# A Fourier-mixing and squared-ReLU feed-forward kernel: from radix 2 to radix 4, with two engines' work moved

## The chip, the cores and the metric

One core of one Trainium2 chip. The metric is the device time of one execution in microseconds (us). Executions of one kernel agree within about 0.3%. A ratio is the mean time of one kernel's fast runs over that of the other's fast runs of the same rounds, so it isn't quite the ratio of the medians that stand beside it; a 95% interval follows it in brackets. Differences to the kernel before are taken within the same rounds.

## The reference

```python
x: (8, 3008, 256) fp32
X = np.fft.fft(np.fft.fft(x, axis=1), axis=2).real    # over the sequence, then over the width
t = X.reshape(24064, 256)
h = np.maximum(t @ w_in, 0.0)                          # w_in  (256, 2048)
out = h * h @ w_out                                    # w_out (2048, 256)
```

## The kernel before

A batch goes through four steps. **Stage 1** multiplies the sequence by cosine and sine tables on the Tensor engine (PE), after the sequence has been split by radix 2 into even and odd rows: two halves of 1504 rows, 12 blocks of 128 each. As 753 output columns are needed and a tile has 384, there are two column tiles, so 16 passes over the 8 batches. **Combine** puts the two halves together with twiddle factors (10 element-wise operations a half on the Vector engine, DVE). **dmix** does the transform over the width on PE. Then come the **feed-forward chains**, 64 in all, of 384 tokens each:

```python
ps_pq   = tile_pool(bufs=4, PSUM)    # stage 1
ps_misc = tile_pool(bufs=2, PSUM)    # dmix, pso
ps_h    = tile_pool(bufs=2, PSUM)    # psh          -> all 8 banks are used
...
for (xt, rev, ...) in chains:                             # 64 times
    h2 = h2p.tile([P, NFC, KT], F16)
    for fc in range(NFC):                                 # 16 "hidden blocks" of 128 hidden units
        psh = ps_h.tile([P, KT], F32)
        for dpc in range(NDC):                            # 2 matmuls, 384 columns
            matmul(psh, win16[...], rhs, ...)
        h1 = h1p.tile([P, KT], F16)                       # 4 buffers
        nc.scalar.activation(h1, psh, AF.Relu)            # ACT, out of PSUM
        nc.vector.tensor_tensor(h2[:, fc, :], h1, h1, op=ALU.mult)      # DVE, square
    for tck in range(ntc):                                # 3 groups of 128 tokens
        pso = ps_misc.tile([P, D], F32)
        for fc in range(NFC):                             # 16 matmuls, 256 columns
            matmul(pso, h2[:, fc, c0 : c0 + P], wout16[:, fc, :], ...)
        nc.scalar.activation(osb, pso, AF.Copy, scale=HS * HS)
        dma(out[...], osb[...])
```

The dmix and feed-forward part of a pass is written after stage 1 of the next one. The order in which PE meets its matmuls isn't the order of this text: it is set when the kernel is built, and it is fixed from then on.

## Time and profile before

| | before |
|---|---|
| time, median | 1118.51 us (13 runs; the four that the prediction had: 1117.62) |
| span, granted PE clock | 1117.4 us, 0.998 |
| PE matmuls: stage 1, dmix, psh, pso | 1536, 256, 2048, 3072 |
| at 0.163 us (384 columns) and 0.115 us (256 columns) | 979 us of pure PE work |
| span less that work | 138 us "lost" |

One view more is needed: the output matmuls (pso) that PE runs in one piece at the end of each feed-forward chain, from the timeline of PE (start in us, duration, group, count).

```profile
566.88 4.26 PE L157 MATMUL pso<-wout,h 128*128 128x256 f16 x35
579.18 4.26 PE L157 MATMUL pso<-wout,h 128*128 128x256 f16 x35
591.49 4.26 PE L157 MATMUL pso<-wout,h 128*128 128x256 f16 x35
```

A chain has 48 pso. In the built order 35 of them stand at the end, so only 13 are left to fill the time in which PE waits for a PSUM buffer of the hidden product. The chains follow each other every 12.30 us, and their own work is 32 x 0.163 + 48 x 0.115 = 10.74 us.

### The profile page before, as it was taken

The numbers are of one execution on the slowest core, as the hardware profiler recorded it, in microseconds if no ns is written. First come the engines' busy times: TensorE is split into PE (matmuls) and PEld (weight loads), VectorE is DVE, ScalarE is ACT, GpSimd is POOL, SyncE is SP. The second block draws the span as 40 slices with busy tenths as digits, with TensorE's granted clock in tenths as the row PEclk, the third lists the DMA queues.
The fourth block names the chain that finished last, engine by engine and source line by source line (L and its number), as shares of the span: only waits on it lengthen the run. The fifth ranks groups of instructions, "written<-read, shape, count | busy, mean of one in ns | idle before, by whom it ended". The sixth has DMA issues, their size and how long they took to land.

```text
span 1117.4 us, 18635 instructions
## 1 busy us (share of the span) xinstructions
PE 1056.5 (95%) x6912; PEld 656.4 (59%) x6912; DVE 633.5 (57%) x1601; ACT 586.2 (52%) x1303; POOL 83.8 (8%) x130
## 2 busy tenths in 40 slices
PE   1699999999999999999999999999999999999998
PEld 0256656666666666656666665656566666665655
DVE  2586564746547474574747456474654747456454
ACT  5537446263653727476262645626365472635666
POOL 5340010100001010020101001010000100000000
PEclk9999999999999999999999999999999999999999
DMA  9062040412304040141403204041221400000101
GB/s 217 6 89 52 30 70 29 71 34 49 55 32 72 28 71 29 35 65 39 69 31 54 47 30 70 28 70 36 47 52 32 67 30 15 28 28 15 37 29 32
DMA packets 78235, 53.63 MB, mean 48 GB/s; under 512 B 3648, under 2 KB 77888, under 8 KB 77888
## 3 DMA queue, kind: packets, MB, share of 16 engines
q0 software_dynamic: 51216, 25.69, 18.0%
q1 hardware_dynamic: 26928, 26.75, 7.2%
q8 instruction: 54, 0.88, 0.3%
q14 instruction: 37, 0.30, 0.1%
HBM read 53.48 MB, written 24.64 MB: 70 GB/s over the span
## 4 chain that ended last, share of the span: by engine, by line
PE 86%; ACT 5%; DVE 4%; issue 2%; POOL 1%; DMA 1%; POOLq 0%; DVEq 0%; ACTq 0%
PE psh L144 33%; PE pso L157 28%; PE ps L211 21%; ACT h L147 3%; DVE h L148 2%; PE psY L128 2%; PE psY L124 2%; DVE m L98 1%; ACT u L92 1%; DMA win<-in_moe_w_in_dram 1%; POOL t L96 1%; ACT eco L102 1%; ACT win L67 0%; DVE xtF L132 0%; POOL t L94 0%
## 5 line engine op out<-in xcount | busy, mean ns | idle before, releaser
L147 ACT ACTIVATE h<-psh 128x384 f16<-128x384 f32 x1024 | 468.3, 490 | 302.9 <-PE psh L144 227.3
L148 DVE TENSOR_TENSOR h<-h 128x384 f16<-128x384 f16 x1024 | 359.4, 358 | 342.7 <-ACT h L147 316.5
L157 PE MATMUL pso<-wout,h 128*128 128x256 f16 x3072 | 478.5, 273 | 8.3 <-DVE h L148 2.2
L157 PEld LDWEIGHTS <-h 128*128 128x128 f16 x3072 | 285.0, 97 | 128.3 <-DVE h L148 34.8
L144 PEld LDWEIGHTS <-win 128*128 128x128 f16 x2048 | 197.7, 97 | 168.8 <-issue 79.7
L144 PE MATMUL psh<-xtF,win 128*128 128x384 f16 x1024 | 231.9, 325 | 8.8 <-ACT h L147 4.3
L144 PE MATMUL psh<-xtR,win 128*128 128x384 f16 x1024 | 231.9, 323 | 5.9 <-ACT h L147 1.0
L160 ACT ACTIVATE osb<-pso 128x256 f32<-128x256 f32 x192 | 73.2, 383 | 176.6 <-PE pso L157 176.5
L211 PEld LDWEIGHTS <-xe 128*128 128x128 f16 (+1 forms) x768 | 76.9, 100 | 74.4 <-DMA xe<-in_x_dram 17.4
L211 PEld LDWEIGHTS <-xo 128*128 128x128 f16 (+1 forms) x768 | 75.5, 98 | 67.2 <-issue 16.4
L211 PE MATMUL ps<-eco,xe 128*128 128x384 f16 (+1 forms) x384 | 76.1, 337 | 30.7 <-ACT eco L102 28.1
L211 PE MATMUL ps<-eco,xo 128*128 128x384 f16 (+1 forms) x384 | 79.5, 332 | 2.9 <-DMA xo<-in_x_dram 2.9
L211 PE MATMUL ps<-esi,xe 128*128 128x384 f16 (+1 forms) x384 | 79.0, 335 | 0.0
L211 PE MATMUL ps<-esi,xo 128*128 128x384 f16 (+1 forms) x384 | 74.6, 332 | 0.0
L189 POOL DMA_DIRECT2D xe<-in_x_dram x16 | 17.4, 1089 | 685.1 <-PE ps L211 566.7
L216 DVE TENSOR_TENSOR t1c<-ps,cbc 128x384 f32<-128x384 f32 x32 | 17.7, 552 | 78.2 <-PE ps L211 77.5
L132 DVE TENSOR_TENSOR xtF<-y1sb,psY 128x384 f16<-128x384 f32 x64 | 35.2, 550 | 6.1 <-PE psY L128 2.6
L131 DVE COPY y1sb<-psY 128x384 f32<-128x384 f32 x64 | 35.1, 549 | 3.5 <-PE psY L124 3.5
L133 DVE TENSOR_TENSOR xtR<-y1sb,psY 128x384 f16<-128x384 f32 x64 | 35.0, 546 | 0.0
L98 DVE SCALAR_TENSOR_TENSOR m<-t,u 128x384 f32<-128x384 f32 (+1 forms) x28 | 15.7, 564 | 29.9 <-POOL t L96 29.9
L92 ACT ACTIVATE u<-krow,mvec 128x384 f32<-128x384 f32 x24 | 14.8, 616 | 27.9 <-DVE m L98 27.9
L218 DVE TENSOR_TENSOR t2c<-ps,sbc 128x384 f32<-128x384 f32 x32 | 17.7, 552 | 13.1 <-PE ps L211 13.1
(47 smaller groups left out, 352.5 us busy)
## 6 DMA issues: line engine op xcount, KB each, us to landing
out_dram<-osb SPq DMA_DIRECT2D x144, 128.0 KB
xe<-in_x_dram POOLq DMA_DIRECT2D x16, 704.0 KB, 7.3
xo<-in_x_dram POOLq DMA_DIRECT2D x16, 704.0 KB, 7.2
win<-in_moe_w_in_dram SPq DMA_DIRECT2D x1, 2048.0 KB
out_dram<-osb SPq DMA_DIRECT2D x16, 127.0 KB
out_dram<-osb SPq DMA_DIRECT2D x16, 113.0 KB
out_dram<-osb SPq DMA_DIRECT2D x16, 112.0 KB
wout<-in_moe_w_out_dram POOLq DMA_DIRECT2D x1, 1024.0 KB, 12.5
```

The costliest lines, as they stand in the source:

```text
L92: nc.scalar.activation(u, src_row, AF.Copy, bias=0.0, scale=scal_ap)
L98: nc.vector.scalar_tensor_tensor(out=m, in0=t2, scalar=-float(nmod), in1=u, op0=ALU.mult, op1=ALU.add)
L124: nc.tensor.matmul(psY1, ccos[:, dc, dpc * P : (dpc + 1) * P], cp[:, dc, :], start=(dc == 0), stop=(dc == NDC - 1))
L131: nc.vector.tensor_copy(y1sb, psY1)
L132: nc.vector.tensor_tensor(xtF[:, dpc, :], y1sb, psY2, op=ALU.subtract)
L133: nc.vector.tensor_tensor(xtR[:, dpc, :], y1sb, psY2, op=ALU.add)
L144: nc.tensor.matmul(psh, win16[:, dpc, fc * P : (fc + 1) * P], rhs, start=(dpc == 0), stop=(dpc == NDC - 1))
L147: nc.scalar.activation(h1, psh, AF.Relu)
L148: nc.vector.tensor_tensor(h2[:, fc, :], h1, h1, op=ALU.mult)
L157: nc.tensor.matmul(pso, h2[:, fc, c0 : c0 + P], wout16[:, fc, :], start=(fc == 0), stop=(fc == NFC - 1))
L160: nc.scalar.activation(osb, pso, AF.Copy, bias=0.0, scale=HS * HS)
L211: nc.tensor.matmul(psu, xs, tabs[mc][0:np_, :], start=(mc == 0), stop=(mc == NMC - 1))
```

## The change

The intent: halve the work of stage 1 by radix 4 (four parts of 752 rows, 6 blocks each, one column tile, 8 passes), and pay for it with a larger combine (8 evictions on ACT and 34 element-wise operations a half), which goes to the idle GpSimd engine (POOL) from the third batch on. Relu and square change engines: relu, out of PSUM, goes to DVE and the square, out of SBUF, to ACT. Room is made with fewer buffers and by giving the fp32 input weights the place of h2.

```diff
-    M = S // 2
+    M = S // R                       # R = 4
...
-    xtp = ...(name="xtp", bufs=5)
+    fsb = ...(name="fsb", bufs=2)
+    gtp = ...(name="gtp", bufs=1)
+    xtp = ...(name="xtp", bufs=9)
...
-    win32 = const.tile([P, NDC, F], F32, name="win32")
+    win32 = h2p.tile([P, NDC, F], F32, name="win32", tag="big")
...
-                nc.scalar.activation(h1, psh, AF.Relu)
-                nc.vector.tensor_tensor(h2[:, fc, :], h1, h1, op=ALU.mult)
+                nc.vector.tensor_scalar(out=h1, in0=psh, scalar1=0.0, scalar2=None, op0=ALU.max)
+                nc.scalar.activation(h2[:, fc, :], h1, AF.Square)
...
-    for kt in range(NKT):            # 2 column tiles
-        for b in range(B):
+    for b in range(B):
...
-                # combine: 10 operations, DVE, out of PSUM
+                for (r, trig), psu in ps4.items():
+                    t_ = fsb.tile([P, KT], F32, ...)
+                    nc.scalar.copy(t_, psu)
...
+            ce = nc.vector if b < 2 else nc.gpsimd
+            for r in range(1, R):
+                m1 = tmp("m1"); ce.tensor_tensor(m1, FC(r), twc[r], op=ALU.mult)
...              # 34 operations in all, two SBUF inputs each
```

More of the change, by code (lines that the diff above doesn't have):

```diff
@@ L16 @@
 HS = 32.0
+RADIX = 4
 def _rev_free_ap(sl: bass.AP, n: int) -> bass.AP:
@@ L36 @@
     P = 128
-    assert S % 2 == 0 and D % P == 0 and F % P == 0
-    M = S // 2
+    R = RADIX
+    assert S % (2 * R) == 0 and D % P == 0 and F % P == 0
+    M = S // R
     KT = 384
@@ L42 @@
     KMAX = M // 2
-    NKT = (KMAX + KT) // KT
+    assert KMAX + 1 <= KT
     NDC = D // P
@@ L50 @@
     xbp = ctx.enter_context(tc.tile_pool(name="xbp", bufs=2))
-    tabp = ctx.enter_context(tc.tile_pool(name="tabp", bufs=3 * (NMC + 1)))
-    krp = ctx.enter_context(tc.tile_pool(name="krp", bufs=2))
+    tabp = ctx.enter_context(tc.tile_pool(name="tabp", bufs=1))
     tgen = ctx.enter_context(tc.tile_pool(name="tgen", bufs=4))
-    cmb = ctx.enter_context(tc.tile_pool(name="cmb", bufs=2))
+    fsb = ctx.enter_context(tc.tile_pool(name="fsb", bufs=2))
+    gtp = ctx.enter_context(tc.tile_pool(name="gtp", bufs=1))
     pqp = ctx.enter_context(tc.tile_pool(name="pqp", bufs=2))
-    xtp = ctx.enter_context(tc.tile_pool(name="xtp", bufs=5))
+    xtp = ctx.enter_context(tc.tile_pool(name="xtp", bufs=9))
+    y1p = ctx.enter_context(tc.tile_pool(name="y1p", bufs=3))
     h1p = ctx.enter_context(tc.tile_pool(name="h1p", bufs=4))
@@ L86 @@
     nc.vector.memset(halfpi, float(math.pi / 2))
-    onec = const.tile([P, 1], F32, name="onec")
-    nc.vector.memset(onec, 1.0)
+    rconst_i = const.tile([P, R], I32, name="rconst_i")
+    nc.gpsimd.iota(rconst_i, pattern=[[1, R]], base=0, channel_multiplier=0)
+    rconst = const.tile([P, R], F32, name="rconst")
+    nc.vector.tensor_copy(rconst, rconst_i)
     def table_pair(src_row, scal_ap, nmod, cos_out, sin_out, ncols):
@@ L106 @@
     csp = const.tile([P, NDC, D], F16, name="csp")
-    csn = const.tile([P, NDC, D], F16, name="csn")
     for dc in range(NDC):
         table_pair(drow, dvec[:, dc : dc + 1], D, ccos[:, dc, :], csp[:, dc, :], D)
-        nc.vector.tensor_scalar(out=csn[:, dc, :], in0=csp[:, dc, :], scalar1=-1.0, scalar2=None, op0=ALU.mult)
-    pending = None
-    y1p = ctx.enter_context(tc.tile_pool(name="y1p", bufs=3))
+    krow_i = const.tile([P, KT], I32, name="krow_i")
+    nc.gpsimd.iota(krow_i, pattern=[[1, KT]], base=0, channel_multiplier=0)
+    krow = const.tile([P, KT], F32, name="krow")
+    nc.vector.tensor_copy(krow, krow_i)
+    eco = []
+    esi = []
+    for mc in range(NMC):
+        tco = tabp.tile([P, KT], F16, name=f"eco{mc}", tag=f"eco{mc}")
+        tsi = tabp.tile([P, KT], F16, name=f"esi{mc}", tag=f"esi{mc}")
+        table_pair(krow, mvec[:, mc : mc + 1], M, tco, tsi, KT)
+        eco.append(tco)
+        esi.append(tsi)
+    twc = [None]
+    tws = [None]
+    for r in range(1, R):
+        c_ = tabp.tile([P, KT], F16, name=f"twc{r}", tag=f"twc{r}")
+        s_ = tabp.tile([P, KT], F16, name=f"tws{r}", tag=f"tws{r}")
+        table_pair(krow, rconst[:, r : r + 1], S, c_, s_, KT)
+        twc.append(c_)
+        tws.append(s_)
     def emit_stage2_dmix(pairs):
@@ L138, in emit_stage2_ffn @@
         for (xt, rev, tb, tok_lo, tok_hi) in chains:
-            h2 = h2p.tile([P, NFC, KT], F16, name="h2", tag="h2")
+            h2 = h2p.tile([P, NFC, KT], F16, name="h2", tag="big")
             for fc in range(NFC):
@@ L163, in emit_stage2_ffn @@
                                       in_=osb[lo : hi + 1, :])
-    for kt in range(NKT):
-        k0 = kt * KT
-        krow_i = krp.tile([P, KT], I32, name="krow_i", tag="krow_i")
-        nc.gpsimd.iota(krow_i, pattern=[[1, KT]], base=k0, channel_multiplier=0)
-        krow = krp.tile([P, KT], F32, name="krow", tag="krow")
-        nc.vector.tensor_copy(krow, krow_i)
-        eco = []
-        esi = []
-        for mc in range(NMC):
-            tco = tabp.tile([P, KT], F16, name=f"eco{mc}", tag="tab")
-            tsi = tabp.tile([P, KT], F16, name=f"esi{mc}", tag="tab")
-            table_pair(krow, mvec[:, mc : mc + 1], M, tco, tsi, KT)
-            eco.append(tco)
-            esi.append(tsi)
-        cbc = tabp.tile([P, KT], F16, name="cbc", tag="tab")
-        sbc = tabp.tile([P, KT], F16, name="sbc", tag="tab")
-        table_pair(krow, onec[:, 0:1], S, cbc, sbc, KT)
-        for b in range(B):
-            xpar = []
-            for par in range(2):
-                xp = xbp.tile([P, NMC, D], F16, name="xe16" if par == 0 else "xo16",
-                              tag="xe16" if par == 0 else "xo16")
-                src = x.rearrange("bb (m two) d -> bb two m d", two=2)[b, par]
-                nc.gpsimd.dma_start(
-                    out=xp[:, 0 : NMC - 1, :],
-                    in_=src[0 : (NMC - 1) * P, :].rearrange("(mc p) d -> p mc d", p=P),
-                )
-                nc.gpsimd.dma_start(out=xp[0:TAILM, NMC - 1, :], in_=src[(NMC - 1) * P : M, :])
-                xpar.append(xp)
-            pa = pqp.tile([P, NDC, KT], F16, name="pa", tag="pa")
-            pb = pqp.tile([P, NDC, KT], F16, name="pb", tag="pb")
-            qa = pqp.tile([P, NDC, KT], F16, name="qa", tag="qa")
-            qb = pqp.tile([P, NDC, KT], F16, name="qb", tag="qb")
-            for dc in range(NDC):
-                if dc == 1 and pending is not None:
-                    pend_xts = emit_stage2_dmix(pending["pairs"])
@@ new lines @@
+    pending = None
+    for b in range(B):
+        xq = []
+        for r in range(R):
+            xp = xbp.tile([P, NMC, D], F16, name=f"x{r}", tag=f"x{r}")
+            src = x.rearrange("bb (m rr) d -> bb rr m d", rr=R)[b, r]
+            nc.gpsimd.dma_start(
+                out=xp[:, 0 : NMC - 1, :],
+                in_=src[0 : (NMC - 1) * P, :].rearrange("(mc p) d -> p mc d", p=P),
+            )
+            nc.gpsimd.dma_start(out=xp[0:TAILM, NMC - 1, :], in_=src[(NMC - 1) * P : M, :])
+            xq.append(xp)
+        pw = [pqp.tile([P, NDC, KT], F16, name=f"pw{t}", tag=f"pw{t}") for t in range(R)]
+        qw = [pqp.tile([P, NDC, KT], F16, name=f"qw{t}", tag=f"qw{t}") for t in range(R)]
+        for dc in range(NDC):
+            fsb_t = {}
+            for grp in range(2):
@@ L203 @@
                 ps4 = {}
-                for par in range(2):
+                for r in (2 * grp, 2 * grp + 1):
                     for trig in range(2):
-                        psu = ps_pq.tile([P, KT], F32, name=f"ps{par}{trig}", tag="pspq")
+                        psu = ps_pq.tile([P, KT], F32, name=f"f{r}{trig}", tag="pspq")
                         tabs = eco if trig == 0 else esi
@@ L209 @@
                             np_ = P if mc < NMC - 1 else TAILM
-                            xs = xpar[par][0:np_, mc, dc * P : (dc + 1) * P]
+                            xs = xq[r][0:np_, mc, dc * P : (dc + 1) * P]
                             nc.tensor.matmul(psu, xs, tabs[mc][0:np_, :],
                                              start=(mc == 0), stop=(mc == NMC - 1))
-                        ps4[(par, trig)] = psu
-                psPE, psQE, psPO, psQO = ps4[(0, 0)], ps4[(0, 1)], ps4[(1, 0)], ps4[(1, 1)]
@@ L215 @@
-                t1c = cmb.tile([P, KT], F32, name="t1c", tag="t1c")
-                nc.vector.tensor_tensor(t1c, psPO, cbc, op=ALU.mult)
-                t2c = cmb.tile([P, KT], F32, name="t2c", tag="t2c")
-                nc.vector.tensor_tensor(t2c, psQO, sbc, op=ALU.mult)
-                uu = cmb.tile([P, KT], F32, name="uu", tag="uu")
-                nc.vector.tensor_tensor(uu, t1c, t2c, op=ALU.subtract)
-                t3c = cmb.tile([P, KT], F32, name="t3c", tag="t3c")
-                nc.vector.tensor_tensor(t3c, psQO, cbc, op=ALU.mult)
@@ L223 @@
-                t4c = cmb.tile([P, KT], F32, name="t4c", tag="t4c")
-                nc.vector.tensor_tensor(t4c, psPO, sbc, op=ALU.mult)
-                vv = cmb.tile([P, KT], F32, name="vv", tag="vv")
-                nc.vector.tensor_tensor(vv, t3c, t4c, op=ALU.add)
-                nc.vector.tensor_tensor(pa[:, dc, :], psPE, uu, op=ALU.add)
-                nc.vector.tensor_tensor(pb[:, dc, :], psPE, uu, op=ALU.subtract)
-                nc.vector.tensor_tensor(qa[:, dc, :], psQE, vv, op=ALU.add)
@@ L230 @@
-                nc.vector.tensor_tensor(qb[:, dc, :], psQE, vv, op=ALU.subtract)
-            if pending is not None:
-                chl = []
-                for (pi, which, tb, tlo, thi) in pending["chains"]:
-                    xt = pend_xts[pi][which]
-                    chl.append((xt, which == 1, tb if which == 0 else tb, tlo, thi))
-                emit_stage2_ffn(chl)
-            bs = b * S
-            k0c = k0
-            desc = {
-                "pairs": [(pa, qa), (pb, qb)],
-                "chains": [
-                    (0, 0, bs + k0c, bs + 0, bs + KMAX),
-                    (1, 0, bs + M + k0c, bs + M, bs + M + KMAX),
-                    (1, 1, bs + M - k0c, bs + M - (KMAX - 1), bs + M - 1),
-                    (0, 1, bs + S - k0c, bs + S - (KMAX - 1), bs + S - 1),
-                ],
-            }
@@ L250, with FC @@
-            pending = desc
+                        ps4[(r, trig)] = psu
+                for (r, trig), psu in ps4.items():
+                    t_ = fsb.tile([P, KT], F32, name=f"fs{r}{trig}", tag=f"fs{r}{trig}")
+                    nc.scalar.copy(t_, psu)
+                    fsb_t[(r, trig)] = t_
+                if grp == 0 and dc == 0 and pending is not None:
+                    pending["xts"] = emit_stage2_dmix(pending["pairs"])
+            def FC(r):
+                return fsb_t[(r, 0)]
@@ new lines, in FS, with tmp @@
+            def FS(r):
+                return fsb_t[(r, 1)]
+            gt = {}
+            def tmp(nm):
+                return gtp.tile([P, KT], F32, name=nm, tag=nm)
+            ce = nc.vector if b < 2 else nc.gpsimd
+            g = {0: (FC(0), FS(0))}
+            for r in range(1, R):
+                m1 = tmp("m1"); ce.tensor_tensor(m1, FC(r), twc[r], op=ALU.mult)
+                m2 = tmp("m2"); ce.tensor_tensor(m2, FS(r), tws[r], op=ALU.mult)
+                grr = tmp(f"grr{r}"); ce.tensor_tensor(grr, m1, m2, op=ALU.subtract)
+                m3 = tmp("m3"); ce.tensor_tensor(m3, FS(r), twc[r], op=ALU.mult)
+                m4 = tmp("m4"); ce.tensor_tensor(m4, FC(r), tws[r], op=ALU.mult)
+                gri = tmp(f"gri{r}"); ce.tensor_tensor(gri, m3, m4, op=ALU.add)
+                g[r] = (grr, gri)
@@ new lines @@
+            e02r = tmp("e02r"); ce.tensor_tensor(e02r, g[0][0], g[2][0], op=ALU.add)
+            d02r = tmp("d02r"); ce.tensor_tensor(d02r, g[0][0], g[2][0], op=ALU.subtract)
+            e13r = tmp("e13r"); ce.tensor_tensor(e13r, g[1][0], g[3][0], op=ALU.add)
+            d13r = tmp("d13r"); ce.tensor_tensor(d13r, g[1][0], g[3][0], op=ALU.subtract)
+            e02i = tmp("e02i"); ce.tensor_tensor(e02i, g[0][1], g[2][1], op=ALU.add)
+            d02i = tmp("d02i"); ce.tensor_tensor(d02i, g[0][1], g[2][1], op=ALU.subtract)
@@ new lines @@
+            e13i = tmp("e13i"); ce.tensor_tensor(e13i, g[1][1], g[3][1], op=ALU.add)
+            d13i = tmp("d13i"); ce.tensor_tensor(d13i, g[1][1], g[3][1], op=ALU.subtract)
+            ce.tensor_tensor(pw[0][:, dc, :], e02r, e13r, op=ALU.add)
+            ce.tensor_tensor(pw[2][:, dc, :], e02r, e13r, op=ALU.subtract)
+            ce.tensor_tensor(qw[0][:, dc, :], e02i, e13i, op=ALU.add)
+            ce.tensor_tensor(qw[2][:, dc, :], e02i, e13i, op=ALU.subtract)
+            ce.tensor_tensor(pw[1][:, dc, :], d02r, d13i, op=ALU.subtract)
@@ new lines @@
+            ce.tensor_tensor(pw[3][:, dc, :], d02r, d13i, op=ALU.add)
+            ce.tensor_tensor(qw[1][:, dc, :], d02i, d13r, op=ALU.add)
+            ce.tensor_tensor(qw[3][:, dc, :], d02i, d13r, op=ALU.subtract)
+        if pending is not None:
+            chl = []
+            for (pi, which, tb, tlo, thi) in pending["chains"]:
+                xt = pending["xts"][pi][which]
+                chl.append((xt, which == 1, tb, tlo, thi))
+            emit_stage2_ffn(chl)
+            pending = None
@@ L252 @@
+        bs = b * S
+        chains = []
+        for t in range(R):
+            chains.append((t, 0, bs + M * t, bs + M * t, bs + M * t + KMAX))
+        for tp_ in range(1, R + 1):
+            chains.append(((R - tp_) % R, 1, bs + M * tp_,
+                           bs + M * tp_ - (KMAX - 1), bs + M * tp_ - 1))
+        pending = {"pairs": [(pw[t], qw[t]) for t in range(R)], "chains": chains}
     if pending is not None:
-        pend_xts = emit_stage2_dmix(pending["pairs"])
+        xts = emit_stage2_dmix(pending["pairs"])
@@ L254 @@
         chl = []
         for (pi, which, tb, tlo, thi) in pending["chains"]:
-            xt = pend_xts[pi][which]
-            chl.append((xt, which == 1, tb, tlo, thi))
+            chl.append((xts[pi][which], which == 1, tb, tlo, thi))
         emit_stage2_ffn(chl)
```

## The prediction

> **What bounds the kernel now.** I read the busy table first, then the chain that ended last, then the groups, then one feed-forward chain of the timeline.
>
> ```profile
> span 1117.4 us, 18635 instructions
> PE 1056.5 (95%) x6912; PEld 656.4 (59%) x6912; DVE 633.5 (57%) x1601; ACT 586.2 (52%) x1303; POOL 83.8 (8%) x130
> PE 86%; ACT 5%; DVE 4%; issue 2%; POOL 1%; DMA 1%; POOLq 0%; DVEq 0%; ACTq 0%
> PE psh L144 33%; PE pso L157 28%; PE ps L211 21%; ACT h L147 3%; DVE h L148 2%; PE psY L128 2%; PE psY L124 2%; DVE m L98 1%; ACT u L92 1%; DMA win<-in_moe_w_in_dram 1%; POOL t L96 1%; ACT eco L102 1%; ACT win L67 0%; DVE xtF L132 0%; POOL t L94 0%
> ```
>
> PE is on the path for 86% of the span. Its three parts are the two feed-forward products (psh and pso) and stage 1 (ps, the cosine and sine sums over the sequence). No other engine is above 57%. POOL is nearly empty, so it can take work. The groups give the durations that I use below:
>
> ```profile
> L147 ACT ACTIVATE h<-psh 128x384 f16<-128x384 f32 x1024 | 468.3, 490 | 302.9 <-PE psh L144 227.3
> L148 DVE TENSOR_TENSOR h<-h 128x384 f16<-128x384 f16 x1024 | 359.4, 358 | 342.7 <-ACT h L147 316.5
> L131 DVE COPY y1sb<-psY 128x384 f32<-128x384 f32 x64 | 35.1, 549 | 3.5 <-PE psY L124 3.5
> L103 ACT ACTIVATE esi<-m 128x384 f16<-128x384 f32 x24 | 12.3, 512 | 8.6 <-PE ps L211 8.6
> L94 POOL TENSOR_SCALAR t<-u 128x384 f32<-128x384 f32 x26 | 13.7, 526 | 40.0 <-ACT u L92 39.5
> ```
>
> "PE busy" does not mean full rate, so I looked for the real rate of a matmul in the chain in order of time. There "3.91 PE ps L211 x24" is 0.163 us for a matmul of 384 columns, and "3.56 PE pso L157 x31" is 0.115 us for one of 256. One feed-forward chain (384 tokens) has 32 psh and 48 pso: 32 x 0.163 + 48 x 0.115 = 10.7 us. But the chains follow each other every 12.30 us (318.15 to 330.45). The other 1.6 us are here:
>
> ```profile
> 320.28 0.48 PE L144 MATMUL psh<-xtR,win 128*128 128x384 f16 x2
> 320.60 0.27 PE L157 MATMUL pso<-wout,h 128*128 128x256 f16 x1
> 320.71 0.49 PE L144 MATMUL psh<-xtR,win 128*128 128x384 f16 x2
> 320.80 2.62 ACT L147 ACTIVATE h<-psh 128x384 f16<-128x384 f32 x5 [0.19 <-PE psh L144]
> 321.04 0.27 PE L157 MATMUL pso<-wout,h 128*128 128x256 f16 x1
> 321.34 0.48 PE L144 MATMUL psh<-xtR,win 128*128 128x384 f16 x2
> ```
>
> Two 128-row groups of psh (two PSUM buffers) take 1.06 us from 320.28 to 321.34, though the PE work in them is 4 x 0.163 + 2 x 0.115 = 0.88 us. It is a loop: fill a buffer (0.48), evict it on ACT (0.49), and about 0.09 for the two handovers. Eight such turns lose 8 x 0.18 = 1.5 us a chain. The order is also not the program's: pso and psh alternate, and stage-1 matmuls of the next batch stand in gaps at a chain's start. So the PE order is filled at build time, and I can't see the new order before it is built.
>
> **What the Trainium skill says.** (1) "VectorE: DVE Perf Modes", section "The perf-mode tier table (the rule you actually need)" and the part on PSUM below it: an fp32 operand in PSUM holds the Vector engine at one element a cycle, for copies and tensor_scalar too. The trace agrees: the copy from PSUM takes 549 ns, as do all its fp32 tensor_tensors (544 to 556), while the f16 square in SBUF takes 358. (2) "GPSIMD Engine Reference", section "Performance versus the Vector engine": a tensor_tensor add of 2048 fp32 is measured at 4497 ns there, 2293 on the Vector engine. No POOL tensor_tensor runs in this kernel, so no row here tests it. (3) "SBUF — State Buffer", section "Who interferes with whom": a Vector instruction with at most one SBUF input, outside the two-port modes, does not contend with GpSimd; one with two SBUF inputs does, when GpSimd reads. No run here shows it yet. (4) "ScalarE: Activation LUTs", section "What ACT_TABLE_LOAD costs": all functions run at the same rate. In the trace, Relu from PSUM takes 490 and Sin from SBUF 512, a difference that can be the source's.
>
> **The change, part by part.**
>
> *Stage 1, radix 2 to 4.* Before: 16 passes (2 column tiles x 8 batches) x 2 x 4 x 12 = 1536 matmuls, the count of its groups. After: 8 passes x 2 x 8 x 6 = 768. The dmix products (8 x 4 pairs x 8 = 256) and the 64 feed-forward chains stay. PE is the path, so 768 x 0.163 = 125 us go. x is read once and not twice, which is worth nothing: DMA is at 26% in the steady window.
>
> *Combine.* Each of 8 x 2 halves gets 8 ACT evictions and 34 element-wise ops. ACT: 128 x 0.49 = 63 us, off the path. For six batches the ops run on POOL. Estimate of one from skill page (2): 4497 x 384/2048 = 843 ns, plus part of a fixed cost that the POOL tensor_scalar suggests (526 at 384 columns, 410 at 256: 0.9 ns a column and about 180 fixed), so 0.85 to 1.05 us. 68 x that is 58 to 71 us a batch, with 8 loads at 0.5 to 1.1 us about 65 to 78. A batch lasts about 120 us on PE, so POOL hides. Its DVE neighbours, relu and the dmix evictions, have at most one SBUF input, so by (3) they don't slow it.
>
> For batches 0 and 1 the 34 ops run on DVE. Back to back, a fp32 op starts every 0.465 us in the timeline (63.52, 63.99, 64.46), so a half costs 34 x 0.465 = 15.8 us and a batch 31.6. In the kernel before, stage 1 of the first pass ends at 47.9 us, held by a table every 2.5 us, and the first psh starts at 80.2. After, 6 tables and not 12 gate it, so it ends its first group near 33. Then the first batch's two combines run on DVE from about 36 to 70, the dmix evictions (24 x 0.465 = 11) to 81, and the second batch's combine (31.6) stands ahead of, or among, the first relus: to 113 if ahead. I take 108 as the effective start of the feed-forward part. That is 28 us later than now. Stage 1 of two passes lies before that point in both kernels, so the 125 us stay whole. One pass's dmix more lies before it: 16 x 0.163 = 2.6 us go.
>
> *Relu to DVE, square to ACT.* The eviction in the PSUM loop becomes 0.55 us and not 0.49: a turn 1.12 to 1.13 and not 1.06, 8 turns a chain, about 0.5 us. The end of a chain's psh phase, where PE now waits 0.49 + 0.37 for relu and square before the last pso, becomes 0.55 + 0.51: up to 0.2 us more. I take 0.6 a chain, 64 x 0.6 = 38 us given back. Throughput isn't the limit: DVE per batch 128 relu + 24 dmix at 0.465 to 0.55 is 71 to 84 us, ACT 128 x 0.51 + 24 x 0.38 + 16 x 0.49 = 82, both under 120.
>
> Sum: 1117.6 - 125 + 28 - 2.6 + 38 = 1056. A steady batch: before 2 x 66.2 = 132.4; after 132.4 - 15.7 + 8 x 0.6 = 121.5. I predict **1052**, a little under the sum, because longer gaps in the loop leave more room for stage-1 matmuls to be filled in.
>
> **Rivals.**
> (a) POOL becomes the bound. For: 34 dependent ops on few temporaries, and the trace shows 0.1 to 0.15 us between dependent POOL ops. It needs over 1.6 us an op (68 x 1.6 + 7 = 116). At 2 us a batch would be 143 us, and six of them make the kernel about 1170. Against: page (2)'s figure is half of that, and the neighbours don't contend. Chance 6%.
> (b) The PSUM loop through DVE costs more: relu, square and pso are in one order on PE, and if each pso waits for its square, a turn can reach 1.3 us. 64 x 8 x 0.18 = 92 us more than the loop now, not 38: about 1105, "within 2%". Against: the order is made at build time and would set pso later. Chance 12%.
> (c) The loop's loss is filled. The PE work of a batch at full rate is 128 x 0.163 + 256 x 0.163 + 384 x 0.115 = 106.8 us. If half of the 15 us loss is filled by stage 1 and other pso, a batch takes 114 us and the kernel about 1000. Chance 15%.
> (d) The start is worse than 28 us: DVE combines, half-rate matmuls (the first full passes run at 0.33 us a matmul until about 55 us) and the feed-forward part queue up. To 60 us: 1085.
>
> **Range and chances.** The sure term is -125; the two given-back terms are 28 (15 to 60) and 38 (0 to 90). Most mixtures end between 1000 and 1098, and I put the range there. "Faster by over 2%" needs under 1095: 0.85. Within 2%: 0.11. Slower: 0.04, only with POOL as the bound.
>
> **What would show it.** Stage-1 groups with 768 matmuls at 0.163 us back to back. POOL tensor_tensor rows at 0.85 to 1.05 us, POOL at 40 to 50% busy; well above 1.2 us says (a), and then dmix matmuls on PE wait for POOL. DVE relu rows near 550 ns, ACT square near 510. The chain of a steady batch with PE still over 80%, turns of the PSUM loop of 1.12 us and chains of 12.8 to 13 us; chains of 14 say (b), of 12 say (c). The first psh after 80 us, with DVE full between 36 and 113 us; a gap of PE there well above 30 us says (d). My number is wrong if the steady batch isn't 118 to 125 us.

## More of the kernel before

Busy shares of a pipelined PE say little, so this text counts matmuls, multiplies by their back-to-back pitch, and calls the rest of the span lost. The prediction shows the busy table, the chain of waits and one stretch of a chain.

## The result, and the profile after

The changed kernel takes 1010.76 us (median of 8 runs, 1010.37 to 1012.24), the kernel before 1118.51: ratio 0.9042 [0.9033, 0.9051]. It is faster by 108 us. That is 41 us less time than the 1052 predicted, and inside the predicted range. From the page after:

```profile
span 1009.6 us, 17366 instructions
PE 932.7 (92%) x6144; PEld 558.9 (55%) x6144; DVE 705.2 (70%) x1380; ACT 644.6 (64%) x1380; POOL 446.5 (44%) x504
PE 81%; DVE 8%; POOL 4%; issue 3%; ACT 2%; DMA 1%; DVEq 0%; ACTq 0%; POOLq 0%
L167 DVE TENSOR_SCALAR h<-psh 128x384 f16<-128x384 f32 x1024 | 536.2, 554 | 229.6 <-PE psh L164 135.0
L168 ACT ACTIVATE h<-h 128x384 f16<-128x384 f16 x1024 | 506.7, 523 | 140.9 <-DVE h L167 135.6
L237 POOL TENSOR_TENSOR grr<-m,m 128x384 f32<-128x384 f32 x36 | 35.9, 998 | 0.1
```

PE has 768 matmuls fewer, as counted. POOL is 44% busy at 0.91 to 1.0 us an operation. PE is still the path, so POOL hides. Relu at 554 ns and square at 523 are as predicted too. So the parts were right, and yet the time is 41 us lower. The ledger says where:

| us | before | after | difference | predicted |
|---|---|---|---|---|
| PE work at full rate | 979 | 854 | -125 | -125 |
| lost until the feed-forward part runs | 46 | 83 | +37 | +25 |
| lost in the rest | 92 | 72 | -20 | +38 (+34 as stated: 1052 for the sum's 1056) |
| span | 1117.4 | 1009.6 | -108 | -62 by its sum, -66 as stated |

For "until the feed-forward part runs" I took, by eye, 80.19 us before, when psh starts in earnest (208 matmuls of 0.163 done, 34 us), and 150 us after (397 matmuls of 0.163 and 22 of 0.115 done, 67 us). The start lost more than predicted. The rest, where the prediction gave time back, gained.

Two views show the gain. First the turn of the PSUM loop, two hidden blocks, in the timelines of PE and of DVE:

```profile
502.25 0.48 PE L164 MATMUL psh<-xtF,win 128*128 128x384 f16 x2
502.57 0.27 PE L177 MATMUL pso<-wout,h 128*128 128x256 f16 x1
502.71 0.49 PE L164 MATMUL psh<-xtF,win 128*128 128x384 f16 x2
503.03 0.52 PE L177 MATMUL pso<-wout,h 128*128 128x256 f16 x3
503.45 0.48 PE L164 MATMUL psh<-xtF,win 128*128 128x384 f16 x2
...
502.84 1.02 DVE L167 TENSOR_SCALAR h<-psh 128x384 f16<-128x384 f32 x2 [0.18 <-ACT h L168]
```

The turn has grown, from 1.06 to 1.20 us (502.25 to 503.45), even more than the 1.12 to 1.13 predicted. But now it holds 1 + 3 pso and not 1 + 1: 4 x 0.163 + 4 x 0.115 = 1.11 us of PE work in 1.20, where it was 0.88 in 1.06. Second, the end of the chains:

```profile
606.99 1.91 PE L177 MATMUL pso<-wout,h 128*128 128x256 f16 x16
618.62 1.91 PE L177 MATMUL pso<-wout,h 128*128 128x256 f16 x16
```

With three pso in half of the waits, only 16 are left for the end, and a chain takes 11.63 us in place of 12.30. Two stage-1 matmuls stand in a chain before and one after (0.163 us each), so a chain loses 12.30 - 10.74 - 0.33 = 1.23 us before and 11.63 - 10.74 - 0.16 = 0.73 after. Over 64 chains that would be 32 us. The ledger has 20, for two reasons. Not every chain reaches 0.73: counted between the starts of the second and the last chain, PE loses 85 us before and 61 after, which is 24 less (25 of the 63 distances between chains are 11.63, the others are longer). And the span runs on for 9.3 us after the last matmul, 3.8 before; the cause of that isn't shown.

The start is the other side. The timelines of DVE, POOL, ACT and PE after:

```profile
117.31 0.54 DVE L257 TENSOR_TENSOR qw<-d02i,d13r 128x384 f16<-128x384 f32 x1
117.78 1.00 DVE L167 TENSOR_SCALAR h<-psh 128x384 f16<-128x384 f32 x2
...
110.51 8.12 POOL L235 TENSOR_TENSOR m<-fs,twc 128x384 f32<-128x384 f32 x1
...
122.20 0.86 ACT L218 COPY fs<-f 128x384 f32<-128x384 f32 x2 [8.47 <-POOL m L239]
...
122.73 2.08 PE L213 MATMUL f<-eco,x 128*128 128x384 f16 x6 [7.19 <-ACT fs L218]
131.78 2.08 PE L213 MATMUL f<-eco,x 128*128 128x384 f16 x6 [5.05 <-ACT fs L218]
134.93 0.85 PE L164 MATMUL psh<-xtF,win 128*128 128x384 f16 x2
```

The first relu waits until 117.78 for the second batch's combine, as feared. But PE doesn't go on with psh then: up to 134.93 it stands in stage-1 matmuls of later batches, which the built order puts ahead of the psh, and waits for ACT to empty their PSUM buffers. ACT in turn waits for one of the two fs buffers (8.47 us in the ACT line), which the combine on POOL holds. The 0.85 us for a pair of psh, 0.48 in the steady part, is the clock: the window from 117.8 to 134.9 was granted 0.66. The Trainium skill, "TensorE: Matmul & The Clock Gate", Part 1 (the clock gate), states that an idle window of about 3.4 us puts the array back to half rate. The trace agrees for the waits of 7.19 and 5.05 us: the six matmuls after each take 2.08 us and not 1.14, and the kernel before, without such waits, was granted 1.00 in this window. It doesn't show 3.4 us as the limit, because after a wait of 2.81 us that ends at 142.49 the grant was 0.50 too.

### The profile page after: what moved, and what is told of

The parts are those of the page before. It is cut to its first block, busy times and chain, and to the rows that moved or that the text cites.

```text
span 1009.6 us, 17366 instructions
## 1 busy us (share of the span) xinstructions
PE 932.7 (92%) x6144; PEld 558.9 (55%) x6144; DVE 705.2 (70%) x1380; ACT 644.6 (64%) x1380; POOL 446.5 (44%) x504
## 4 chain that ended last, share of the span: by engine, by line
PE 81%; DVE 8%; POOL 4%; issue 3%; ACT 2%; DMA 1%; DVEq 0%; ACTq 0%; POOLq 0%
PE psh L164 35%; PE pso L177 35%; PE f L213 7%; PE psY L148 2%; PE psY L144 2%; DVE h L167 2%; DMA win<-in_moe_w_in_dram 1%; DVE xtF L152 1%; ACT h L168 1%; POOL t L99 1%; POOL t L101 1%; DVE xtR L153 1%; DVE m L235 0%; DVE grr L237 0%; DVE m L236 0%
## 5 line engine op out<-in xcount | busy, mean ns | idle before, releaser
L167 DVE TENSOR_SCALAR h<-psh 128x384 f16<-128x384 f32 x1024 | 536.2, 554 | 229.6 <-PE psh L164 135.0
L168 ACT ACTIVATE h<-h 128x384 f16<-128x384 f16 x1024 | 506.7, 523 | 140.9 <-DVE h L167 135.6
L177 PE MATMUL pso<-wout,h 128*128 128x256 f16 x3072 | 515.5, 274 | 6.7 <-ACT h L168 4.2
L218 ACT COPY fs<-f 128x384 f32<-128x384 f32 x128 | 59.7, 477 | 128.7 <-PE f L213 67.8
L213 PEld LDWEIGHTS <-x 128*128 128x128 f16 (+1 forms) x768 | 78.7, 102 | 109.7 <-issue 54.0
L235 POOL TENSOR_TENSOR m<-fs,twc 128x384 f32<-128x384 f32 x36 | 40.1, 1115 | 216.9 <-ACT fs L218 216.7
L213 PE MATMUL f<-eco,x 128*128 128x384 f16 (+1 forms) x384 | 94.5, 350 | 40.8 <-ACT fs L218 20.8
L213 PE MATMUL f<-esi,x 128*128 128x384 f16 (+1 forms) x384 | 93.3, 347 | 8.2 <-ACT esi L108 8.2
L237 POOL TENSOR_TENSOR grr<-m,m 128x384 f32<-128x384 f32 x36 | 35.9, 998 | 0.1
L240 POOL TENSOR_TENSOR gri<-m,m 128x384 f32<-128x384 f32 x36 | 35.9, 998 | 0.0
```

Of the source, the lines that this page charges most:

```text
L167: nc.vector.tensor_scalar(out=h1, in0=psh, scalar1=0.0, scalar2=None, op0=ALU.max)
L168: nc.scalar.activation(h2[:, fc, :], h1, AF.Square)
L177: nc.tensor.matmul(pso, h2[:, fc, c0 : c0 + P], wout16[:, fc, :], start=(fc == 0), stop=(fc == NFC - 1))
L213: nc.tensor.matmul(psu, xs, tabs[mc][0:np_, :], start=(mc == 0), stop=(mc == NMC - 1))
L218: nc.scalar.copy(t_, psu)
L235: m1 = tmp("m1"); ce.tensor_tensor(m1, FC(r), twc[r], op=ALU.mult)
```

## The experiments

My theory after the result: the gain in the rest is the built order of PE (more pso in each turn), and the engines' exchange gained only through it. Rivals: the exchange itself made the loop better; the move of the combine to POOL relieved DVE; or the loop is as bad as ever and stage 1 fills it. The twelve runs:

| run | time, us | ratio to before |
|---|---|---|
| changed kernel | 1010.76 | 0.9042 [0.9033, 0.9051] |
| swap_only | 1103.61 | 0.9881 [0.9864, 0.9897] |
| noswap | 1245.05 | 1.1145 [1.1128, 1.1163] |
| fused_before | 1119.84 | 1.0019 [1.001, 1.0029] |
| pool_from1 | 1013.78 | 0.9075 [0.9062, 0.9089] |
| lag3_before | 1050.36 | 0.9403 [0.9388, 0.9418] |
| lag3_after | 1006.69 | 0.9008 [0.8993, 0.9023] |
| dve_all | 1019.56 | 0.9124 [0.9111, 0.9138] |
| fsb3 | 999.38 | 0.8942 [0.8929, 0.8956] |
| h1_8 | 1010.32 | 0.9044 [0.9029, 0.9059] |
| lag3_fsb3_h6 | 998.79 | 0.8938 [0.8921, 0.8954] |
| lag3_ph3 | 978.39 | 0.8753 [0.8739, 0.8768] |
| lag3_dve_old | 951.54 | 0.8517 [0.8504, 0.853] |

All gave correct results.

### The engines' exchange alone (swap_only)

The kernel before, with the two lines of relu and square as in the changed kernel, and nothing else.

> The kernel before, radix 2 and all, with only relu moved to DVE and square to ACT. Order theory: the build fills each turn of the PSUM loop with 1+3 output matmuls (it placed 1+1 before), so a chain goes from 12.3 to about 11.6 us and the kernel to about 1075 us (1065 to 1090). Rival, the step of the prediction: a longer eviction costs 0.6 us a chain, about 1156 us.

It took 1103.61 us, 14 less than before: under 2%, but clear of the noise. PE's timeline at the ends of two chains:

```profile
300.08 1.91 PE L157 MATMUL pso<-wout,h 128*128 128x256 f16 x16
311.72 1.91 PE L157 MATMUL pso<-wout,h 128*128 128x256 f16 x16
```

The chain is that of the changed kernel, 11.64 us with 16 pso at its end. So the exchange alone brings the other order, and the loss that the prediction put on the exchange (38 us; this run would then have been slower than before, not faster) is refuted. But the whole pass shrank from 66.2 only to 65.2 us, so my size for this run was too good. Of the 0.67 us a chain, 0.16 is a stage-1 matmul that now stands elsewhere. And in the first chain of a pass PE loses 1.66 us, 1.32 before; DVE has relu (554 ns for the square's 358) besides the combine there and is 74% busy for 57%.

### The change without the exchange (noswap)

```diff
-                nc.vector.tensor_scalar(out=h1, in0=psh, scalar1=0.0, scalar2=None, op0=ALU.max)
-                nc.scalar.activation(h2[:, fc, :], h1, AF.Square)
+                nc.scalar.activation(h1, psh, AF.Relu)
+                nc.vector.tensor_tensor(h2[:, fc, :], h1, h1, op=ALU.mult)
```

> The changed kernel with relu back on ACT and square back on DVE; radix 4 and the POOL combine stay. Order theory: the order falls back to 1+1 output matmuls a turn and 35 at the end, chains of 12.3 us, about 1051 us. Rival (the shorter chains come from radix 4 or from the combine leaving DVE): stays at 1011, within 10. Beside that: the square reads two SBUF inputs on DVE, so POOL tensor_tensors should grow from about 0.95 us, to 1.1 to 1.5; if they pass 1.6 us POOL holds PE and the time rises above 1070.

1245.05 us, 234 more than the changed kernel and 128 more than the kernel before: a clear miss. The order fell back to 35 pso at the end, but that is the small part. The timelines of DVE, POOL and PE show the large one:

```profile
356.87 15.47 DVE L168 TENSOR_TENSOR h<-h 128x384 f16<-128x384 f16 x1 [0.41 <-ACT h L167]
...
357.06 0.92 POOL L236 TENSOR_TENSOR m<-fs,tws 128x384 f32<-128x384 f32 x1
...
371.14 0.98 POOL L257 TENSOR_TENSOR qw<-d02i,d13r 128x384 f16<-128x384 f32 x1
...
372.40 0.66 PE L177 MATMUL pso<-wout,h 128*128 128x256 f16 x2 [14.64 <-DVE h L168]
```

One square, 0.36 us elsewhere, takes 15.47 us on DVE. It begins with a run of 16 POOL operations and ends with it, and PE stands for 14.64 us. Nine squares are held like this, for 1.5 to 44.5 us; the two longest lie beside 48 POOL operations each. Another 137 take 0.6 to 1.2 us and come in between POOL operations one by one. What decides between the two isn't shown. In all PE waits 171 us for squares. The square's mean is 583 ns here; with the same square and no POOL combine it is 355 (lag3_dve_old, below). I had expected POOL to be the one that slows down. So the exchange, which leaves no operation with two SBUF inputs on DVE in the chains, isn't a detail of the loop: with relu and square in their old places the POOL combine costs far more than the 9 us that it saves beside the exchange (dve_all, below).

### The even order, two ways (fused_before, lag3_before)

If the order is the cause, the old engines must gain from it. In fused_before the pso of two of the three token groups stand in the hidden loop, right behind the square; in lag3_before three hidden blocks later:

```diff
                 nc.vector.tensor_tensor(h2[:, fc, :], h1, h1, op=ALU.mult)
+                if fc >= 3:                             # fused_before: no lag, "fc" and no "if"
+                    for tck in range(NIL):              # NIL = 2 of 3 token groups
+                        out_mm(tck, fc - 3, psos[tck])
+            for fc in range(NFC - 3, NFC):              # lag3_before only
+                for tck in range(NIL):
+                    out_mm(tck, fc, psos[tck])
```

> The kernel before with relu on ACT and square on DVE as they were, but the output matmuls of two of the three column blocks written inside the loop over the hidden blocks, so that the build interleaves 32 of the 48 and leaves 16 at the end. Order theory: the order alone gives the gain, chains of 11.4 to 11.8 us, 1070 to 1090 us. Rival (the engines of relu and square matter, not the order): 1118 within 10.

> The kernel before, engines of relu and square as before, two of the three output column blocks written inside the hidden loop as in the run that gave nothing, but three hidden blocks behind, so that the built order is an even 2 psh, 2 pso and no pso stands right behind its square. Order theory, mended: what counts is output matmuls in every turn that are ready when PE reaches them; a turn costs its PE work, 1.11 us, chains about 11.2 us with no stage-1 in them, an iteration about 63 us and not 66.2, the kernel 1065 to 1085 us. Rival (the engines, not the order): 1118 within 10.

fused_before: 1119.84 us, no gain. Its pso stand too close to their squares: the weight load of pso waited 146 us for the square (35 in the kernel before), and ACT 336 us for psh (227 before). lag3_before: 1050.36 us, 67 less than before, with no other change and no matmul saved. Its PE timeline:

```profile
303.75 0.49 PE L152 MATMUL psh<-xtR,win 128*128 128x384 f16 x2
304.08 0.38 PE L145 MATMUL pso<-wout,h 128*128 128x256 f16 x2
304.30 0.49 PE L152 MATMUL psh<-xtR,win 128*128 128x384 f16 x2
```

A hidden block every 0.545 us, which is its own work (2 x 0.163 + 2 x 0.115 = 0.556, so PE waits for nothing), and a chain of 10.84 us for 12.30. This settles the main question: on the old engines the order alone is worth 67 us. What a chain loses falls from 1.23 us to 10.84 - 10.74 = 0.10.

### The same order in the changed kernel, and what holds its turn (lag3_after, h1_8, lag3_ph3)

> The changed kernel with the same even order, three blocks behind. Order theory: the turn falls from 1.206 us towards its PE work of 1.11, chains 11.2 to 11.4 and not 11.63, so 64 x 0.3 = about 20 us less, 985 to 1000 us. Rival: the turn is held by relu, square and the h1 buffer (0.55 + 0.52 + handovers = 1.2 us) whatever the order, 1011 within 6.

Only 4 us: 1006.69. The psh pairs in PE's timeline stand at

```profile
501.61 0.48 PE L172 MATMUL psh<-xtF,win 128*128 128x384 f16 x2
...
502.15 0.48 PE L172 MATMUL psh<-xtF,win 128*128 128x384 f16 x2
...
502.81 0.48 PE L172 MATMUL psh<-xtF,win 128*128 128x384 f16 x2
```

0.54 and 0.66 us apart by turns, so two blocks still take 1.20 us, and the chain 11.64, though the order is even. The trace put the wait of relu down to ACT ("0.18 <-ACT h" in the DVE line above), so I took the free h1 buffer, which relu must wait for, as the cause, and doubled it:

```diff
-    h1p = ctx.enter_context(tc.tile_pool(name="h1p", bufs=4))
+    h1p = ctx.enter_context(tc.tile_pool(name="h1p", bufs=8))
```

> The changed kernel with eight buffers for h1 in place of four; nothing else, and the built order of PE keeps its 1 and 3 output matmuls a turn. If the turn of 1.206 us is held by the free h1 buffer that relu waits for (the slot), twice as many let relu run ahead, the turn falls to the matmuls' own 1.11 to 1.13 us, a chain to about 11.0 to 11.2 us, and the kernel to 975 to 995 us. If it is held by a round trip through the square and the two PSUM buffers (relu on DVE at 554 ns twice a turn plus handovers), the buffers change nothing: the turn stays at 1.2 us and the kernel within 1005 to 1015 us.

1010.32 us, nothing. The DVE timeline of this run:

```profile
501.74 1.02 DVE L167 TENSOR_SCALAR h<-psh 128x384 f16<-128x384 f32 x2 [0.18 <-ACT h L168]
502.94 1.02 DVE L167 TENSOR_SCALAR h<-psh 128x384 f16<-128x384 f32 x2 [0.18 <-ACT h L168]
```

The same wait of the same 0.18 us, so the releaser named there is not the cause; the psh that relu reads was done only 0.1 us earlier. What fits is the round trip of one PSUM buffer in the turn shown above: psh from 502.25 to 502.73, relu at 502.84 (0.11 later) to 503.39, the next psh into that buffer at 503.45 (0.06 later). 0.48 + 0.11 + 0.55 + 0.06 = 1.20. With ACT as the reader it was 0.48 + 0.49 + 0.09 = 1.06: the two handovers take 0.17 us with DVE and 0.09 with ACT (the profile models PE's ends, so their sum is surer than its parts). To test it I gave psh a third PSUM buffer, from stage 1, in lag3_after:

```diff
-    ps_pq = ...(name="ps_pq", bufs=4, space=PSUM)
+    ps_pq = ...(name="ps_pq", bufs=3, space=PSUM)
-    ps_h = ...(name="ps_h", bufs=2, space=PSUM)
+    ps_h = ...(name="ps_h", bufs=3, space=PSUM)
```

> The changed kernel with the even order (output matmuls three hidden blocks late) and three PSUM buffers for the hidden product in place of two; stage 1 gives one of its four (three). Eight h1 buffers changed nothing, so the h1 buffer doesn't hold the turn. The theory left: the turn is the round trip of one PSUM buffer, filled in 0.48 us, a handover of 0.11, relu 0.55, a handover of 0.06, together 1.20 us for two hidden blocks. With a third buffer three blocks share a round trip of 1.2 us, so PE's own work sets the pace: 0.555 us a block and not 0.60, a chain near 11.0 us and not 11.64, and the kernel 40 us shorter than with the even order alone (1006.69): 960 to 980 us. Rival: relu on the Vector engine can't go faster than 0.60 us a block whatever the buffers, or the loss of a stage-1 buffer costs as much: 1000 to 1015 us.

978.39 us, 28 less than lag3_after, and PE's timeline has the pace of its own work, 0.545 us a block and 11.02 us a chain:

```profile
508.84 0.49 PE L172 MATMUL psh<-xtR,win 128*128 128x384 f16 x2
...
509.39 0.49 PE L172 MATMUL psh<-xtR,win 128*128 128x384 f16 x2
...
509.93 0.49 PE L172 MATMUL psh<-xtR,win 128*128 128x384 f16 x2
```

A chain is 0.62 us shorter, of which 0.16 is a stage-1 matmul that left it: what a chain loses falls from 11.64 - 10.74 - 0.16 = 0.74 to 11.02 - 10.74 = 0.28 us, and 63 x 0.46 is 29 us, which is the gain. The start is as before, with 67 us of PE work done by 150 us in both runs. That the round trip through two PSUM buffers causes the long turn is shown.

### The start and the engine of the combine (pool_from1, fsb3, dve_all)

Three runs vary the changed kernel's start and its POOL combine: pool_from1 takes POOL from the second batch on (`b < 1`), fsb3 gives fs a third buffer, with the weights loaded in two halves to make room, and dve_all leaves the combine on DVE for every batch.

```diff
+            ce = nc.vector if b < 1 else nc.gpsimd                     # pool_from1
+            ce = nc.vector                                             # dve_all
+    fsb = ctx.enter_context(tc.tile_pool(name="fsb", bufs=3))          # fsb3
+        win32 = h2p.tile([P, F], F32, name="win32", tag="big")         # fsb3, for each half c
```

> The changed kernel with only the first batch's combine on DVE; from the second on POOL. Start theory: the second batch's 31.6 us on DVE and POOL's blocked first operation leave the path of the first relu, the feed-forward part runs from about 90 us and not 143, and the kernel takes 980 to 1000 us. Rival: the start only shifts stage-1 work, PE is full later anyway, 1011 within 5.

> The changed kernel with three buffers and not two for the evicted stage-1 sums (the 16 KB load of the first weights is cut in two to make the room). Start theory: at the start PE stands 4 to 7 us at a time at stage-1 matmuls whose PSUM can't be evicted until a combine frees a buffer; a third one takes about 10 to 20 us off, 990 to 1002. Rival: the combines' own time (DVE, then POOL) sets the start, a third buffer only moves the wait, 1011 within 4.

> The changed kernel with every combine on DVE. Theory: 31.6 us more DVE work a batch, 78 + 32 = 110 of 113 us, in runs of 16 us in which no relu and no dmix eviction is done; PE waits for most of each, 1060 to 1130 us. Rival (PE hides it behind stage 1 and pso as it hides the rest): 1011 within 10.

pool_from1: 1013.78 us, 3 more. The stage-1 matmuls ahead of psh now wait for the slower POOL combine, 19.51 us in one piece, and 269 of them are done by 150 us, not 335; with the psh and pso, PE has done 67 us of work by then in both runs. Taking the combine from DVE doesn't help a start whose order puts PE behind the combine anyway.

fsb3: 999.38 us, 11 less. Its three longest waits at the start, 5.03, 6.20 and 3.25 us, are hardly shorter than 3.90, 7.19 and 5.05, but PE has done 78 us of work by 150 us and not 67. So 11 of the start's 37 us go with this run's two edits, the third fs buffer and the split load; no run separates them, and 2 of the 11 us are there by 50 us already.

dve_all: 1019.56 us, only 9 more than the changed kernel, a miss of mine. The 9 is what two larger parts leave. At the start dve_all is better: its built order lets PE go on with psh at 117.96 and not at 134.93,

```profile
117.96 0.95 PE L164 MATMUL psh<-xtF,win 128*128 128x384 f16 x4 [2.83 <-DVE h L167]
```

and PE has done 86 us of work by 150 us and not 67. After that the ledger's loss is 100 us and not 73, with DVE 85% busy. So the move to POOL costs 19 us at the start and gains 27 later: a net 8 us of the span, 9 of the time. The 19 us are about half of the start's 37, and the prediction had not counted them there.

### Putting it together (lag3_fsb3_h6, lag3_dve_old)

> The three edits at once: even order of the output matmuls three hidden blocks late, three fs buffers, six h1 buffers (three output buffers, to make room). If h1's buffer holds the turn, even order and start together give 955 to 985 us. If it doesn't, only what the order (4 us) and the start (11 us) gave alone adds up: 994 to 998 us.

Even order, three fs buffers, six h1 buffers in the changed kernel: 998.79 us. That is fsb3 again; the 4 us of the order and the 11 of the start did not fully add.

As the exchange costs a longer round trip and, once the order is set by hand, is needed only because POOL combines, and as POOL is worth only 9 us, I undid both and kept radix 4:

```diff
-                nc.vector.tensor_scalar(out=h1, in0=psh, scalar1=0.0, scalar2=None, op0=ALU.max)
-                nc.scalar.activation(h2[:, fc, :], h1, AF.Square)
+                nc.scalar.activation(h1, psh, AF.Relu)
+                nc.vector.tensor_tensor(h2[:, fc, :], h1, h1, op=ALU.mult)
...
-            ce = nc.vector if b < 2 else nc.gpsimd
+            ce = nc.vector
                                        # and: pso three blocks late, three fs buffers
```

> Radix 4 with the old engines: relu back on ACT, square back on DVE, the whole combine on DVE (no POOL), even order three blocks late, three fs buffers. If the even turn of the kernel before (0.545 us a hidden block, a chain of 10.84 us) survives, the steady batch is 8 x 10.84 plus what of stage 1 and dmix isn't hidden (about 13 to 18 us): 100 to 105 us, and the kernel 930 to 965 us. Rival: the DVE queue is in order, and the combine's 34 operations of a half (16 us) stand between squares: PE then waits for h at each half, up to 10 us twice a batch, and the kernel ends at 1000 to 1080 us.

951.54 us, 59 less than the changed kernel and 165 less than the kernel before. Its busy line and two chain ends:

```profile
PE 889.0 (94%) x6144; PEld 585.1 (62%) x6144; DVE 693.9 (73%) x1788; ACT 625.6 (66%) x1381; POOL 59.7 (6%) x96
567.73 1.91 PE L166 MATMUL pso<-wout,h 128*128 128x256 f16 x16
578.57 1.91 PE L166 MATMUL pso<-wout,h 128*128 128x256 f16 x16
```

The chain is 10.84 us, as in lag3_before. DVE has the whole combine and is still busy for less time (693.9 us) than in the changed kernel (705.2), because a square costs it 355 ns and a relu out of PSUM 554. The rival's waits exist (DVE is on 32% of the chain of waits, 8% after): 30 of the 63 distances between chains are 10.84, and other chains inside a batch take up to 12.1 us. fsb3 has the same fs buffers and takes 48 us more. About 20 of these are the start (98 us of PE work done by 150 us, 78 in fsb3) and about 29 the rest. Order, exchange and the combine's engine differ at once between these two runs, so their shares aren't shown. Of the expectation, the time (930 to 965) and the chain came out.

## Why the prediction was right or wrong

The verdict (faster by over 2%) and the range held; the number was 41 us too high. Its two misses had opposite signs, 12 us at the start and 58 in the rest, so the total came out nearer than its worse part: that is luck.

- **Stage 1, -125: right.** 768 matmuls went, and the ledger's work term is -125.
- **The combine on POOL: right in size and in effect.** 0.91 to 1.0 us an operation for 0.85 to 1.05 predicted, POOL 44% busy for 40 to 50, hidden. The Trainium skill, "SBUF — State Buffer", "Who interferes with whom", states that a Vector instruction with at most one SBUF input, outside the two-port modes, doesn't contend with GpSimd. The trace agrees for relu: 554 ns with and without a POOL operation beside it. But noswap shows that I had not seen what rested on it: without the exchange the kernel takes 234 us more, the worse order included.
- **The start, +28 - 2.6: right in mechanism, too small.** Measured +37. "I take 108 as the effective start" took DVE's queue as the end of it. The first relu ran at 117.78, and PE's order kept psh back until 134.93. The missing part was stage 1 of later batches ahead of psh, held by two fs buffers (11 us by fsb3, with the split load), by the POOL combine of the third batch (about 19 us by dve_all, with its order; the two overlap) and a clock of 0.66. Rival (d) named the direction.
- **"Relu to DVE, square to ACT ... I take 0.6 a chain, 64 x 0.6 = 38 us given back": this step failed.** Measured: about 20 us gained. Two things were wrong in it. The turn was taken as 0.48 + 0.55 + 0.09; the handovers are 0.17 with DVE, so it is 1.20 us (shown by the trace, and by lag3_ph3, which removes it). That would have made it worse. The larger one: the step held what fills a turn constant, one pso a block. The new built order puts 1 + 3 in it and leaves 16 for the end, and a chain became 0.67 us shorter (0.50 without the stage-1 matmul that moved). swap_only shows that order without the rest of the change; lag3_before shows the order's worth without the exchange, 67 us.
- **Rivals.** (c), "the loop's loss is filled", is what happened, and it put the kernel at about 1000; I gave it 15%. It named stage 1 and other pso as the filler; in the chains shown it was pso alone, and one stage-1 matmul fewer. (a) and (b) did not occur: POOL isn't the bound, and pso don't wait for their squares in the turn.
- **The test it set itself** (the number is wrong if a steady batch isn't 118 to 125 us, "chains of 12 say (c)") answered: chains are 11.63, and eight of them, a batch, take 107 to 116 us from the second batch to the sixth. So the number is wrong by its own test.

The prediction did say that the order is made at build time and can't be seen before. It then used the old order in its sum. That is the fault to learn from, more than the 0.08 us.

What stays open: why the build picks 1 + 3 for one pair of engines and 1 + 1 for the other. No run has the exchange with the old order, so what the longer turn alone would have cost is not measured. And no run has the POOL combine without the exchange in the even order.

## What to carry to other kernels

When a change moves work between the engines of a loop with two PSUM buffers, compute the turn as fill, handover, read, handover, and then count what the built order puts into it: the filler is worth more than 0.1 us of an eviction, and it can be set by hand (lag3_before: 67 us for moving the consumer three blocks back, with no work saved). Ask of each part of a change what it is there for: here the exchange was needed for the POOL combine, POOL was worth 9 us, and the order that the exchange brought could be set by hand. Radix 4 with neither, in the even order and with a third fs buffer, was the fastest of the runs. And don't trust a releaser in the trace until you have removed it: the h1 buffer was named and was innocent.

## What the Trainium skill lacked or had wrong

- "SBUF — State Buffer", "Who interferes with whom": it has the rule for two SBUF inputs and says that issue order decides who blocks, but states the exclusive hold for one instruction only. Here one side that runs back to back can keep the other out for many instructions: single DVE squares took 15.47 us beside 16 POOL operations and 44.53 beside 48 (noswap, kernel 1245.05 us), and one POOL operation took 8.12 us (0.91 elsewhere) until DVE's run of combine operations ended (changed kernel; 9.06 in pool_from1). In the same noswap trace ten squares took turns with POOL operations, 10.72 us for all. When which happens is on no page that I read.
- "GPSIMD Engine Reference", "Performance versus the Vector engine": it gives 4497 ns for 2048 columns only. At 384 columns fp32 the runs have 0.91 to 1.0 us an operation (0.87 to 0.96 from start to start), above the 843 ns that the prediction estimated by scaling.
- No page that I read has the handovers of a PSUM loop: psh to relu to psh took 0.17 us beyond the two durations with DVE as the reader and 0.09 with ACT.
- No page that I read says that the order in which a build places PE's instructions decides how much of such a loop is filled: 35 or 16 pso at the chain's end, 12.30 or 10.84 us a chain, 1118 or 1050 us (lag3_before).
